# A fused sketched attention and feed-forward kernel: GpSimd's queue, the key products and the task list rearranged

## The chip, the core and the metric

The kernel runs on one core of a Trainium2 chip. Such a core has five engines with a queue of instructions each: PE (TensorE, matrix products), DVE (VectorE), ACT (ScalarE), POOL (GpSimd) and SP (SyncE, which here only issues DMAs). Sixteen DMA engines move data between HBM and the on-chip memory SBUF; PE writes its results to PSUM, which only DVE and ACT read here. The metric is the device time of one execution in microseconds (us), lower is better.

## What is computed

Two parts, one after the other. The attention is linear: each query and key row of 32 numbers is multiplied by two small sketches S1 and S2 (8 x 32), and its 64 features are all products of the 8 numbers of the one with the 8 of the other.

```python
def phi(x):                                        # x: (4, 4, 1088, 32), batch, head, row, 32
    a = einsum('rd,bhsd->bhsr', S1, x)             # 8 numbers per row
    b = einsum('rd,bhsd->bhsr', S2, x)
    return einsum('bhsi,bhsj->bhsij', a, b)        # 64 features
kv  = einsum('bhsf,bhsd->bhfd', phi(k), v)
z   = sum(phi(k), axis=rows)
num = einsum('bhsf,bhfd->bhsd', phi(q), kv)
den = einsum('bhsf,bhf->bhs',  phi(q), z) + 1e-6
x   = (num / den), as 4352 tokens of 4 heads x 32 = 128
h   = x @ w_in                                     # 128 -> 2048
out = (h * sigmoid(h)) @ w_out                     # 2048 -> 128
```

Inputs and output are f32. The second part has 4352 x 2048 silus and two products of 4352 x 128 x 2048.

## The kernel before

The program is a list of small tasks. `ORDER`, a text of entries such as `pk 0 2 4` or `f1 3 5`, names them in the order in which they are written into the program, and each engine works through its own instructions in that order; nothing reorders them. An engine waits at an instruction until all that it depends on is done, and what is behind it waits too. The DMA loads and a few memsets are not in the list: they are written ahead of it, and so stand first in the queues of SP, ACT and POOL.

The attention of each batch b (0 to 3) goes through these tasks. Keys: `kt b` transposes K on DVE; `pk` multiplies by the sketch weights WK on PE; `tk` transposes the result back into SBUF (tile `pk`); `kp b e h` forms the 64 products per key, in four steps of 128 x 576 elements (tile `kp`), all on DVE. `zs`, `zc`, `mm`, `mk` sum the features and put the denominator's weights into a part of the tile WQ. `kv` is the key-value product on PE (with V in bf16, tile `Vb`), and `kw` (on ACT for batch 0, as `kw_act`) masks it by head into KVw. Queries, in pieces of p0 to p1: `qt` transposes, `pq` multiplies by WQ on PE, `tq` transposes back into PQ, `dn` forms and divides by the denominator (four short DVE instructions), `qo` forms the 64 products, `pt` transposes them, `nm` multiplies by KVw on PE, and `xc` copies the attention's result to `xT`, 128 features by token, on ACT (A) or DVE (V).

The feed-forward part goes over ten chunks of tokens (`CHUNKS`: 256, 384, 448, six of 512 and 192). Chunks 0 to 2 are batch 0. `f1 c s` multiplies w_in with a chunk for two (or four, or eight) of the 16 blocks of 128 columns, `sl c s` is the silu on ACT, `f2 c s` adds up the product with w_out in PSUM, and `ot c` transposes and stores. There are two PSUM buffers for `f1` (an H in the list lets a task of the attention use one). `wic i` casts a quarter of w_in to bf16 on ACT, `vc0` casts batch 0's V. `zeros n` are n matrix products with a tile of zeros that nobody reads; they fill PE's time in the start.

`WQ`'s other columns are constants: `wq_const` copies WK into the WQ of the four batches, eight copies on POOL. `L4`, the matrix of `mm`, is made in `weights2`, on DVE.

Loads: K, the first queries and V of batch 0, w_in and the remaining queries are issued by SP without a condition. w_out and V of batches 1 to 3 are issued by POOL, since they are cast to bf16 on the way. `begin(..., after)` makes an issue wait until another transfer has landed:

```python
wo = begin(nc.gpsimd, w_out_bf, moe_w_out.rearrange("(j p) m -> p j m", p=P), wi[1])
prev = q0b
for b in range(1, B):
    load_v(nc.gpsimd, b, Vb[b], prev)
    kb = load_kq(nc.sync, b, k, Kx, after=prev)
    prev = load_kq(nc.sync, b, q, Qx, after=kb)
```

So each K and Q load of batches 1 to 3 is issued when the one before it has landed, and POOL issues the V of a batch when the queries of the batch before have landed.

Of the kernel before, what the change touches and what calls it, by code (L numbers as in the profile page):

```python
# [26 lines left out]
tq 0 10 17, f2 0 0, qo 0 4 10, f1 0 2, pt 0 4 10, sl 0 2
pk 1, dn 0 10 17, nm 0 4 10 H, tk 1, xc 0 4 10 A, kt 2 0 34
f2 0 1, f2 0 2, qo 0 10 17, f1 1 0, sl 1 0, f1 1 4
zs 1, f1 1 2, sl 1 4, f2 0 3, f1 1 1, zc 1 A  # L30
pk 2, sl 1 2, ot 0, pt 0 10 17, sl 1 1, f1 1 6
qt 1 0 34, f2 1 0, f1 1 3, tk 2, mm 1, f2 1 1
sl 1 6, f1 1 5, f2 1 2, mk 1, kp 1 0 1, nm 0 10 17
sl 1 3, pq 1 0 8 H, kp 1 1 1, sl 1 5, xc 0 10 17 A, tq 1 0 8
kp 1 0 0, f1 1 7, kp 1 1 0, f2 1 3, pq 1 8 17, f1 2 0
dn 1 0 8, f2 1 4, sl 1 7, f1 2 4, sl 2 0, kv 1
# [53 lines left out]
def kernel(  # L90
# [157 lines left out]

    def wq_const():
        for b in range(B):  # L250
            nc.gpsimd.tensor_copy(out=WQ[b][:, :, 0:R].rearrange("p h (i e) -> p h e i", e=2),
                                  in_=WK[:, :, 0, :].rearrange("p h (e i) -> p h e i", e=2))
            nc.gpsimd.tensor_copy(out=WQ[b][:, :, R: 2 * R], in_=WK[:, :, 1, :])  # L253

# [26 lines left out]
    def kp(b, e, h):  # L281
        s = t["pk", b][:, :, :, h].rearrange("p n r a i -> p (n r) a i")
        o = t["kp", b][:, :, :, e, h].rearrange("p n r j i -> p (n r) j i")
        nc.vector.tensor_tensor(out=o, in0=bcast(s[:, :, 0, 4 * e: 4 * e + 4], 2, R),  # L284
                                in1=bcast(s[:, :, 1], 3, 4), op=ALU.mult)
# [221 lines left out]
```

## Time and profile before

| | us |
|---|---|
| time, median of 3 runs (range) | 122.09 (121.97 to 122.43) |
| the profiled execution's own time | 121.77 |
| its span, first to last instruction | 119.1 |
| busy: PE, ACT, DVE, POOL | 88.3, 73.3, 67.6, 12.1 |
| 72 silus on ACT, busy | 65.5 |
| 16 key product steps (`kp`) on DVE, busy | 11.3 |
| mean granted TensorE clock | 0.912 of full |

Line numbers such as L352 are those of the kernel before. A row of the timeline gives start, duration, engine, line, operation, the tile written and the tile read with their shapes, the number of instructions that were merged into it, and in brackets how long the engine had stood idle before it and what ended the idle time. A row of the waits gives who waited for whom, the sum in us, how often, and the longest. A row of the groups (line first) gives busy us and the mean duration in ns. A row of the windows gives the stretch, its length, the busy time and the number of instructions of PE, its weight loads, DVE, ACT and POOL, then clock, share of the DMA engines and GB/s. Rows of DMA issues give KB and the us from issue to landing.

### The profile page before, as it was taken

Reading aid. Unit: us, or ns where it says so; the run is one execution under the profiler, and the core shown is the slowest. Engines: PE = TensorE matmul, PEld = TensorE weight load, DVE = VectorE, ACT = ScalarE, POOL = GpSimd, SP = SyncE. Lnnn points to the kernel's source line nnn. Section 1 sums busy time; section 2 is a strip of 40 time slices with the busy share of each in tenths; the row PEclk is TensorE's granted clock in tenths of the full one; section 3 lists DMA queues with packets and bytes.
Section 4 is the critical chain, followed back from the end, with each engine's and each line's share of the span. In section 5 each row is a group of like instructions: output and inputs, shape, how many; then the busy total and the mean of one; then the engine's idle time right before and its main releaser. Section 6 shows DMA issues by size and latency. Waiting matters only on the chain.

```text
span 119.1 us, 2189 instructions
## 1 busy us (share of the span) xinstructions
PE 88.3 (74%) x857; PEld 48.1 (40%) x864; DVE 67.6 (57%) x128; ACT 73.3 (62%) x91; POOL 12.1 (10%) x47
## 2 busy tenths in 40 slices
PE   6499000000089999999999999999999999999920
...
DVE  0349300000048999999999999799398973020210
ACT  2217300000004779969879988999989789999800
...
PEclk9999975555558999999999999999999999999999
...
GB/s 99 288 265 279 125 277 122 151 243 195 148 192 129 6 0 0 44 6 3 66 6 19 61 0 0 90 3 0 88 0 6 47 41 70 18 1 67 21 102 22
DMA packets 24857, 9.81 MB, mean 82 GB/s; under 512 B 21392, under 2 KB 23184, under 8 KB 24848
## 3 DMA queue, kind: packets, MB, share of 16 engines
...
q8 instruction: 6, 0.10, 0.3%
q10 hardware_dynamic: 288, 0.03, 0.2%
q14 instruction: 3, 0.02, 0.1%
...
## 4 chain that ended last, share of the span: by engine, by line
PE 42%; DMA 23%; DVE 17%; ACT 8%; issue 2%; SPq 2%; POOL 2%; POOLq 0%; ACTq 0%; DVEq 0%
PE o_ps L437 18%; PE h_ps L419 16%; DMA Qx<-in_q_dram 11%; DMA Kx<-in_k_dram 9%; ACT g L426 8%; DVE qp L378 3%; DMA T<-in_S_dram 3%; DVE kp L284 2%; DVE PQ L358 2%; PE zps L236 2%; DVE KT L258 2%; SPq L157 2%; POOL Vb L157 2%; PE pq_ps L352 2%; DVE qT L384 1%
## 5 line engine op out<-in xcount | busy, mean ns | idle before, releaser
L426 ACT ACTIVATE g<-h_ps 128x1024 bf16<-128x1024 f32 (+2 forms) x72 | 65.5, 981 | 7.8 <-PE h_ps L419 5.7
L419 PE MATMUL h_ps<-xT,w_in_bf 128*128 128x512 bf16 (+4 forms) x156 | 39.8, 347 | 0.5
L437 PE MATMUL o_ps<-g,w_out_bf 128*128 128x512 bf16 (+4 forms) x157 | 37.5, 346 | 0.4
L437 PEld LDWEIGHTS <-w_out_bf 128*128 128x128 bf16 x160 | 15.2, 98 | 14.5 <-issue 0.7
L419 PEld LDWEIGHTS <-w_in_bf 128*128 128x128 bf16 x160 | 14.2, 98 | 15.2 <-issue 5.6
L352 PE MATMUL pq_ps<-QT,WQ 64*64 64x288 f32 (+3 forms) x48 | 4.0, 409 | 21.6 <-POOL WQ L253 21.6
L358 DVE STREAM_TRANSPOSE PQ<-pq_ps 128x576 f32<-128x576 f32 (+3 forms) x6 | 4.0, 669 | 23.0 <-PE pq_ps L352 23.0
L335 ACT ACTIVATE KVw<-kv_ps,hm 64x64 bf16<-64x64 f32 (+1 forms) x6 | 1.5, 306 | 22.8 <-PE kv_ps L316 22.7
L443 DVE STREAM_TRANSPOSE o_tt<-o_ps 128x512 f32<-128x512 f32 (+4 forms) x10 | 6.3, 635 | 13.9 <-PE o_ps L437 13.8
L236 PE MATMUL zps<-zw 128*128 128x128 bf16 x112 | 10.7, 264 | 1.1 <-POOL hm L196 1.1
L284 DVE TENSOR_TENSOR kp<-pk 128x576 bf16<-128x576 f32 x16 | 11.3, 740 | 0.0
L352 PEld LDWEIGHTS pq_ps<-QT,WQ 64*64 64x64 f32 x48 | 1.4, 143 | 23.4 <-POOL WQ L253 21.7
L236 PEld LDWEIGHTS <-zw 128*128 128x128 bf16 x112 | 9.0, 123 | 3.7 <-issue 2.5
L378 DVE TENSOR_TENSOR qp<-PQ 128x1024 bf16<-128x1024 f32 (+4 forms) x9 | 10.3, 1146 | 0.1
L157 POOL DMA_DIRECT2D Vb<-in_v_dram x12 | 6.5, 546 | 15.2 <-DMA Qx<-in_q_dram 15.2
L384 DVE STREAM_TRANSPOSE qT<-qp 128x512 f32<-128x512 f32 (+4 forms) x9 | 5.9, 659 | 0.1
L258 DVE STREAM_TRANSPOSE KT<-Kx 128x1088 f32<-128x1088 f32 (+2 forms) x5 | 5.3, 1063 | 0.0
L341 DVE STREAM_TRANSPOSE QT<-Qx 128x1088 f32<-128x1088 f32 (+2 forms) x5 | 5.3, 1057 | 0.0
L230 ACT ACTIVATE Vb<-Vx 128x576 bf16<-128x576 f32 x2 | 1.3, 675 | 5.0 <-DMA Vx<-in_v_dram 5.0
L227 DVE CAST xT<-num_ps 128x576 bf16<-128x576 f32 (+1 forms) x5 | 3.6, 714 | 0.2
L271 PE MATMUL h_ps<-KT,WK 64*32 64x288 f32 x16 | 2.4, 682 | 1.8 <-DVE hm L245 1.8
L316 PEld LDWEIGHTS <-kp 128*128 128x128 bf16 x72 | 3.1, 107 | 0.7 <-DVE kp L284 0.2
...
## 6 DMA issues: line engine op xcount, KB each, us to landing
...
w_out_bf<-in_moe_w_out_dram POOLq DMA_DIRECT2D x1, 512.0 KB, 7.0
...
```

The source lines that it names most:

```text
L157: ins = eng.dma_start(dst, src)
L236: nc.tensor.matmul(t["zps"][:, :ncol], zw, zw[:, :ncol], start=True, stop=True)
L258: nc.vector.transpose(out=KT[b % 2][:, y0 * 32: y1 * 32], in_=Kx[b][:, y0:y1, :].rearrange("p a d -> p (a d)"))
L284: nc.vector.tensor_tensor(out=o, in0=bcast(s[:, :, 0, 4 * e: 4 * e + 4], 2, R), in1=bcast(s[:, :, 1], 3, 4), op=ALU.mult)
L352: nc.tensor.matmul(t["pq_ps", b, p0][64 * g: 64 * (g + 1), r, :cols].rearrange("p (y x) -> p y x", x=32), w[rs, :], qv[rs, g, p0:p1, :], s ...
L358: nc.vector.transpose(out=PQ[b % 2][:, p0:p1].rearrange("p y r f -> p r y f"), in_=t["pq_ps", b, p0][:, :, :cols].rearrange("p r (y f) -> ...
L378: nc.vector.tensor_tensor(out=t["qp", b][:, p0:p1].rearrange("p y r j i -> p (y r) j i"), in0=bcast(fa, 2, R), in1=bcast(fb, 3, R), op=ALU ...
L384: nc.vector.transpose(out=dst.rearrange("p r (y x) -> p y r x", x=32), in_=src)
L419: nc.tensor.matmul(h[:, i, :], w_in_bf[:, j * P: (j + 1) * P], xT[:, t0: t0 + ntok], start=True, stop=True)
L426: nc.scalar.activation(out=gv, in_=t.pop(("h", c, s)), func=ACT.Silu)
L437: nc.tensor.matmul(op[c][:, :ntok], w_out_bf[:, j, :], g[:, i, :], start=(j == 0), stop=(j == NJ - 1))
L443: nc.vector.transpose(out=o_tt[:, :ntok], in_=op[c][:, :ntok])
```

## The change

- POOL's queue: V of batches 1 to 3 and w_out are no longer issued ahead of the list, but by tasks in it (`lv b`, `wo`). `wo` waits only for batch 0's V; `lv` for nothing of its own.
- SP: K and Q of batches 1 to 3 are issued without a condition, right behind batch 0's. (The program has eight completion counters for such transfers, used in turn, so an issue waits for the transfer that had its counter before.)
- 11 of the 16 `kp` steps get a P in the list, and run on POOL: two of batch 0, four each of batches 1 and 2, one of batch 3.
- `L4` is made on POOL. The sketches are loaded into 32 rows (T16: two copies of S1 and of S2), and four transposes of 32 x 32 spread them over the partitions; a copy of S2 on all partitions (T2) is kept for L4.
- w_out is loaded with four consecutive rows (2 KB) per partition and group, and w_in's columns are read with a step of four in `wic`, so that the blocks of the two still match.
- The list is another one. `zc` of batch 0 and 1 and `kw` of batch 0 go from ACT to DVE; `zeros` have other counts.

The core of the diff (of the task list, two lines):

```diff
-kp 0 1 1, zeros 13, zs 0, kp 0 0 0, zc 0 A, kp 0 0 1
+kp 0 0 1 P, kp 0 1 1 P, zeros 6, pq 0 0 4, zeros 15, kv 0
...
-    T12 = const.tile([P, 2, D], FP32, name="T12")
-    ST = const.tile([P, 2, 4, R], FP32, name="ST")
+    T16 = const.tile([32, D], FP32, name="T16")
+    T2 = const.tile([P, D], FP32, name="T2")
+    ST = const.tile([P, 2, 2, R], FP32, name="ST")
...
-    sketch(nc.scalar, 0, S1)
-    sketch(nc.scalar, 1, S2)
+    sketch(nc.scalar, T16[0:16, :], S1, 2)
+    sketch(nc.scalar, T16[16:32, :], S2, 2)
...
+    sketch(nc.scalar, T2, S2, P // R)
+    v0 = load_v(nc.sync, 0, Vx)
     for i in range(4):
-        wi.append(begin(nc.sync, w_in_f[:, i * CH:(i + 1) * CH], moe_w_in[:, i * CH:(i + 1) * CH]))
-    q0b = load_kq(nc.sync, 0, q, Qx, 8, NY)
+        begin(nc.sync, w_in_f[:, i * CH:(i + 1) * CH], moe_w_in[:, i * CH:(i + 1) * CH])
+    load_kq(nc.sync, 0, q, Qx, 8, NY)
+    for b in range(1, B):
+        load_kq(nc.sync, b, k, Kx)
+        load_kq(nc.sync, b, q, Qx)
...
-    wo = begin(nc.gpsimd, w_out_bf, moe_w_out.rearrange("(j p) m -> p j m", p=P), wi[1])
-    prev = q0b
-    for b in range(1, B):
-        load_v(nc.gpsimd, b, Vb[b], prev)
-        kb = load_kq(nc.sync, b, k, Kx, after=prev)
-        prev = load_kq(nc.sync, b, q, Qx, after=kb)
...
     def weights():
-        vcopy_in = T12.rearrange("p a d -> p (a d)")
-        nc.vector.transpose(out=ST.rearrange("p a c i -> p (a c i)"), in_=vcopy_in)
-        nc.vector.tensor_tensor(out=WK, in0=ST[:, :, 0:2, :].rearrange("p a h i -> p h a i"),
+        for i in range(4):
+            nc.vector.transpose(out=ST[32 * i: 32 * (i + 1)].rearrange("p a h i -> p (a h i)"), in_=T16)
+        nc.vector.tensor_tensor(out=WK, in0=ST.rearrange("p a h i -> p h a i"),
...
-        nc.vector.tensor_tensor(out=L4, in0=bcast(T12[:, 1, :], 1, H), in1=bcast(hm4, 2, D),
-                                op=ALU.mult)
+        nc.gpsimd.tensor_tensor(out=L4, in0=bcast(T2, 1, H), in1=bcast(hm4, 2, D), op=ALU.mult)
...
+    def wo():
+        begin(nc.gpsimd, w_out_bf.rearrange("p (i e) m -> p i (e m)", e=4),
+              moe_w_out.rearrange("(i p e) m -> p i (e m)", p=P, e=4), v0)
+
+    def lv(b):
+        load_v(nc.gpsimd, b, Vb[b])
...
-    def kp(b, e, h):
+    def kp(b, e, h, eng=nc.vector):
...
-        nc.vector.tensor_tensor(out=o, in0=bcast(s[:, :, 0, 4 * e: 4 * e + 4], 2, R),
+        eng.tensor_tensor(out=o, in0=bcast(s[:, :, 0, 4 * e: 4 * e + 4], 2, R),
...
-    def wic(i, n=4):
-        w = DFF // n
-        acopy(w_in_bf[:, i * w: (i + 1) * w], w_in_f[:, i * w: (i + 1) * w])
+    def wic(i):
+        cols = slice(i * CH, (i + 1) * CH)
+        acopy(w_in_bf[:, cols].rearrange("p (e m) -> p e m", e=4),
+              w_in_f[:, cols].rearrange("p (m e) -> p e m", e=4))
...
-    named = {"A": acopy, "V": vcopy}
+    named = {"A": acopy, "V": vcopy, "P": nc.gpsimd}
```

POOL's queue, right behind its memsets, before. Vb_91 to Vb_93 are V of batches 1 to 3, WQ_98 is batch 0's WQ; a bracket names the counters of the engines and transfers that the instruction waits for (DMAHW transfers of SP and ACT, DMASW those of POOL):

```order
L157 DMA w_out_bf<-in_moe_w_out_dram 128x16x128 [waits DMAHW2_49]
L157 DMA Vb_91<-in_v_dram 32x4x288 [waits DMAHW5_49]
L157 DMA Vb_91<-in_v_dram 32x4x288 x2
L157 DMA Vb_91<-in_v_dram 32x4x224
L157 DMA Vb_92<-in_v_dram 32x4x288 [waits DMAHW7_49]
L157 DMA Vb_92<-in_v_dram 32x4x288 x2
L157 DMA Vb_92<-in_v_dram 32x4x224 [waits DMASW0_49]
L157 DMA Vb_93<-in_v_dram 32x4x288 [waits DMAHW1_49,DMASW1_49]
L157 DMA Vb_93<-in_v_dram 32x4x288 [waits DMASW2_49]
L157 DMA Vb_93<-in_v_dram 32x4x288 [waits DMASW3_49]
L157 DMA Vb_93<-in_v_dram 32x4x224 [waits DMASW4_49]
L251 COPY WQ_98<-WK 128x2x2x4 [waits DVE_49,Pool_49]
```

The same place now; kp_229, kp_483 and kp_564 are the products of batches 0, 1 and 2 (between the first copies and the last stand those of the other WQ):

```order
L242 TENSOR_TENSOR L4_120<-T2_117,hm4_123 128x128 [waits DMAHW4_49,DVE_49,Pool_49]
L246 COPY WQ0_98<-WK_119 128x2x2x4
L248 COPY WQ0_98<-WK_119 128x2x8
...
L286 TENSOR_TENSOR kp_229<-pk_228 128x18x32 [waits DVE_49]
L286 TENSOR_TENSOR kp_229<-pk_228 128x18x32
L158 DMA w_out_bf_114<-in_moe_w_out_dram 128x4x512 [waits DMAHW1_49]
L158 DMA Vb1_91<-in_v_dram 32x4x288 x3
L158 DMA Vb1_91<-in_v_dram 32x4x224
L158 DMA Vb2_92<-in_v_dram 32x4x288 x3
L158 DMA Vb2_92<-in_v_dram 32x4x224 [waits DMASW0_49]
L286 TENSOR_TENSOR kp_483<-pk_482 128x18x32 [waits DVE_49]
L286 TENSOR_TENSOR kp_483<-pk_482 128x18x32 x3
```

The copies into WQ moved from behind all twelve V loads to ahead of every load, behind L4; two product steps stand ahead of w_out, and the V of batch 3 (not shown) behind all eleven.

DVE's queue from the key products of batch 0 to the first use of its KVw, before (PQ_106 is the transposed query product; `kw` of this batch was on ACT):

```order
L284 TENSOR_TENSOR kp<-pk 128x18x32 x3
L306 TENSOR_TENSOR WQ_98<-m_ps,hm_120 128x2x2x4
L284 TENSOR_TENSOR kp<-pk 128x18x32
L358 STREAM_TRANSPOSE PQ_106<-pq_ps 128x2x4x32
L368 TENSOR_TENSOR AW_108<-PQ_106 128x8x8
L369 TENSOR_REDUCE DN_110<-AW_108 128x8
L370 RECIPROCAL DN_110<-DN_110 128x8
L371 TENSOR_TENSOR PQ_106<-PQ_106,DN_110 128x8x8
L341 STREAM_TRANSPOSE QT_96<-Qx_85 128x832
L378 TENSOR_TENSOR qp<-PQ_106 128x512
L384 STREAM_TRANSPOSE qT<-qp 128x4x2x32
L358 STREAM_TRANSPOSE PQ_106<-h_ps 128x2x6x32
```

And now, from the second product step on:

```order
L286 TENSOR_TENSOR kp<-pk 128x18x32
L308 TENSOR_TENSOR WQ_98<-m_ps,hm_121 128x2x2x4
L360 STREAM_TRANSPOSE PQ_106<-pq_ps 128x2x4x32
L370 TENSOR_TENSOR AW_108<-PQ_106 128x8x8
...
L380 TENSOR_TENSOR qp<-PQ_106 128x512
L386 STREAM_TRANSPOSE qT<-qp 128x4x2x32
L327 TENSOR_TENSOR KVw_102<-kv_ps,hm_121 128x128
L330 TENSOR_TENSOR KVw_102<-kv_ps,hm_121 64x128 x2
L343 STREAM_TRANSPOSE QT_96<-Qx_85 128x832
L223 CAST xT<-num_ps 128x256
L360 STREAM_TRANSPOSE PQ_106<-h_ps 128x2x6x32
```

Two of the four product steps left DVE's queue here; the three masks of `kw` and the copy of `xc` came in, and the long transpose of the remaining queries moved behind them.

More of the change, by code (lines that the diff above doesn't have):

```diff
@@ L27 @@
[L27 to L36, printed above, removed]
@@ L78 @@
-ot 8, f2 9 0, f2 9 1, sl 9 3, f2 9 2, f2 9 3
-ot 9
+weights, vc0 0 2, vc0 2 4, kt 0 0 18, kt 0 18 34, qt 0 0 8
+zeros 33, pk 0 0 2 H, zeros 3, pk 0 2 4, weights2, tk 0
+wq_const, kp 0 0 0, zeros 13, zs 0, zc 0 V, zeros 5
+mm 0, wic 1, wic 0, kp 0 1 0, mk 0, wic 2
+kp 0 0 1 P, kp 0 1 1 P, zeros 6, pq 0 0 4, zeros 15, kv 0
+tq 0 0 4, dn 0 0 4, qo 0 0 4, pt 0 0 4, kw 0, zeros 23
+nm 0 0 4, qt 0 8 34, wic 3, xc 0 0 4 V, wo, zeros 11
+pq 0 4 10 H, f1 0 0, tq 0 4 10, dn 0 4 10, qo 0 4 10, sl 0 0
+pq 0 10 17, f1 0 1, zeros 2, f1 0 2, pt 0 4 10, f2 0 0
@@ new lines @@
+dn 1 0 8, f1 2 1, f1 2 0, sl 2 1, mm 2, kp 2 0 1 P
+pk 3, kp 2 1 1 P, sl 2 0, f1 2 4, f2 1 6, f1 2 3
+mk 2, sl 2 4, kp 2 0 0 P, qo 1 0 8, tk 3, sl 2 3
+kv 1, f1 2 7, sl 2 7, kw 1, pt 1 0 8, f2 1 7
+f1 2 2, pq 1 8 17, nm 1 0 8 H, ot 1, xc 1 0 8 V, zs 3
+sl 2 2, kp 2 1 0 P, tq 1 8 17, f1 2 6, f2 2 0, f1 3 0
+f2 2 1, f2 2 2, sl 2 6, sl 3 0, f1 3 2, sl 3 2
+qt 2 0 34, f2 2 3, dn 1 8 17, f1 2 5, pq 2 0 8, sl 2 5
+f1 3 6, f2 2 4, sl 3 6, kp 3 0 0, f1 3 7, qo 1 8 17
+zc 3 V, f2 2 5, sl 3 7, pt 1 8 17, tq 2 0 8, f2 2 6
@@ new lines @@
+f1 3 1, sl 3 1, f2 2 7, ot 2, f1 3 4, sl 3 4
+kv 2, f1 3 5, f2 3 0, nm 1 8 17 H, sl 3 5, pq 2 8 17
+f1 3 3, dn 2 0 8, f2 3 1, xc 1 8 17 V, f1 4 1, f2 3 2
+sl 3 3, kw 2, f1 4 0, qo 2 0 8, kp 3 1 1 P, sl 4 1
+f2 3 3, pt 2 0 8, f1 4 4, kp 3 0 1, sl 4 0, f2 3 4
+f1 4 3, sl 4 4, sl 4 3, f2 3 5, f2 3 6, f1 4 7
+f2 3 7, tq 2 8 17, sl 4 7, f1 4 6, sl 4 6, mm 3
+nm 2 0 8, ot 3, f1 4 2, sl 4 2, f2 4 0, f1 4 5
+qt 3 0 34, f2 4 1, lv 3, xc 2 0 8 V, f1 5 4, sl 4 5
+f2 4 2, f2 4 3, sl 5 4, mk 3, f1 5 0, f2 4 4
@@ new lines @@
+sl 5 0, f1 5 5, dn 2 8 17, pq 3 0 8, qo 2 8 17, pt 2 8 17
+kp 3 1 0, sl 5 5, f1 5 2, f2 4 5, f1 5 6, f2 4 6
+sl 5 2, tq 3 0 8, sl 5 6, nm 2 8 17, f1 5 1, dn 3 0 8
+f2 4 7, sl 5 1, f1 5 3, sl 5 3, xc 2 8 17 V, pq 3 8 17
+f1 6 2, ot 4, sl 6 2, tq 3 8 17, f2 5 0, f1 5 7
+f2 5 1, sl 5 7, f2 5 2, f1 6 0, sl 6 0, dn 3 8 17
+f2 5 3, f2 5 4, qo 3 8 17, f1 6 5, f2 5 5, qo 3 0 8
+f1 6 6, sl 6 5, kv 3, kw 3, f1 6 7, pt 3 0 8
+f2 5 6, sl 6 6, f1 6 1, f2 5 7, sl 6 7, ot 5
+f1 6 4, nm 3 0 8, sl 6 1, xc 3 0 8 V, sl 6 4, f1 6 3
```

85 lines of the change are left out of this document (28 added, 57 removed).

## Prediction

> **What bounds the kernel now.** I read the slices first, to see whether one engine is the limit all the way, then the waits, then the timeline around the longest one. On the page, each digit is a fortieth of the span, 2.98 us:
>
> ```profile
> span 119.1 us, 2189 instructions
> PE   6499000000089999999999999999999999999920
> DVE  0349300000048999999999999799398973020210
> ACT  2217300000004779969879988999989789999800
> PEclk9999975555558999999999999999999999999999
> ```
>
> All three engines stand still in slices 5 to 10. After that PE is full to slice 38. The kernel is thus 39 us of start and 75 us of dense work, and the start is mostly a hole. The waits name what closes it:
>
> ```profile
> PE pq_ps L352 <- POOL WQ L253: 21.6, 1, 21.6
> POOL Vb L157 <- DMA Qx<-in_q_dram: 15.2, 3, 7.9
> ```
>
> The first query product (`pq`, L352) wants the constant columns of WQ, copied by GpSimd (POOL). The timeline shows why the copies are late:
>
> ```profile
> 9.15 0.78 DVE L278 STREAM_TRANSPOSE pk<-h_ps 128x576 f32<-128x576 f32 x1 [1.86 <-PE h_ps L271]
> 9.91 1.29 POOL L157 DMA_DIRECT2D w_out_bf<-in_moe_w_out_dram  x1 [5.56 <-DMA w_in_f<-in_moe_w_in_dram]
> 9.97 2.10 DVE L284 TENSOR_TENSOR kp<-pk 128x576 bf16<-128x576 f32 x3
> 11.98 0.17 DVE L306 TENSOR_TENSOR WQ<-m_ps,hm 128x16 f32<-128x16 f32 x1
> 12.59 2.16 POOL L157 DMA_DIRECT2D Vb<-in_v_dram  x4 [1.38 <-DMA Qx<-in_q_dram]
> ...
> 30.71 2.15 POOL L157 DMA_DIRECT2D Vb<-in_v_dram  x4 [5.90 <-DMA Qx<-in_q_dram]
> 32.90 0.20 POOL L251 COPY WQ<-WK 128x16 f32<-128x16 f32 x1
> 33.28 0.70 PE L352 MATMUL pq_ps<-QT,WQ 64*64 64x128 f32 x8 [21.57 <-POOL WQ L253]
> ```
>
> The copies stand in GpSimd's queue behind twelve V loads, and those wait for the chain of K and Q loads. DVE's own part of WQ was done at 12.15. The chain of work shows the loads one behind the other (544 KB each):
>
> ```profile
> 12.30 6.78 DMA Kx<-in_k_dram
> 19.10 3.28 DMA Qx<-in_q_dram
> ```
>
> The dense part, from the first `f1` to the end:
>
> ```profile
> 39.23 1.04 PE L419 MATMUL h_ps<-xT,w_in_bf 128*128 128x256 bf16 x8
> 39.87 3.77 ACT L426 ACTIVATE g<-h_ps 128x1024 bf16<-128x1024 f32 x4 [0.70 <-PE h_ps L419]
> 59.22 0.68 DVE L227 CAST xT<-num_ps 128x512 bf16<-128x512 f32 x1
> 59.96 0.38 PE L419 MATMUL h_ps<-xT,w_in_bf 128*128 128x512 bf16 x1
> 71.60 0.69 PE L316 MATMUL kv_ps<-Vb,kp 128*128 128x64 bf16 x18
> 113.93 0.38 DVE L443 STREAM_TRANSPOSE o_tt<-o_ps 128x192 f32<-128x192 f32 x1 [1.70 <-PE o_ps L437]
> ```
>
> Batch 0 (chunks 0 to 2) is worked off from 39.23 to 59.96, 20.7 us, while DVE makes batch 1; the rest takes 119.1 - 59.96 = 59.1 us.
>
> **The hole.** Now the copies follow `L4` on GpSimd, which needs the sketches and one DVE reduction: both are there by 8 us (pk itself is transposed at 9.15), and eight copies of 0.20 end before DVE's part of WQ. No load stands ahead of them. The chain that sets the first `f1` is then DVE's, and its steps have these durations:
>
> ```profile
> 34.05 0.45 DVE L358 STREAM_TRANSPOSE PQ<-pq_ps 128x256 f32<-128x256 f32 x1 [21.24 <-PE pq_ps L352]
> 34.54 0.22 DVE L368 TENSOR_TENSOR AW<-PQ 128x64 f32<-128x64 f32 x1
> 35.51 1.04 DVE L341 STREAM_TRANSPOSE QT<-Qx 128x832 f32<-128x832 f32 x1
> 36.47 0.65 DVE L378 TENSOR_TENSOR qp<-PQ 128x512 bf16<-128x512 f32 x1
> 37.16 0.45 DVE L384 STREAM_TRANSPOSE qT<-qp 128x256 f32<-128x256 f32 x1
> 37.29 0.56 PE L352 MATMUL h_ps<-QT,WQ 64*64 64x192 f32 x8
> 38.79 0.39 ACT L230 ACTIVATE xT<-h_ps 128x256 bf16<-128x256 f32 x1 [1.67 <-PE h_ps L393]
> L325 DVE TENSOR_TENSOR KVw<-kv_ps,hm 128x128 bf16<-128x128 f32 x3 | 0.8, 263 | 0.0
> L328 DVE TENSOR_TENSOR KVw<-kv_ps,hm 64x128 bf16<-64x128 f32 x6 | 1.7, 289 | 0.2
> ```
>
> The four steps of the quotient (`dn`) take 35.51 - 34.54 = 0.97.
>
> **A key product step on GpSimd.** No row shows it: 576 elements, two operands read, one written. The nearest rows:
>
> ```profile
> L284 DVE TENSOR_TENSOR kp<-pk 128x576 bf16<-128x576 f32 x16 | 11.3, 740 | 0.0
> L207 POOL MEMSET Vx<- 32x256 f32 x1 | 0.3, 307 | 0.1
> L196 POOL MEMSET hm<- 128x2 f32 x1 | 0.1, 101 | 0.0
> L251 POOL COPY WQ<-WK 128x16 f32<-128x16 f32 x4 | 0.8, 200 | 0.0
> L203 POOL TENSOR_SCALAR_AFFINE_SELECT E<-E 128x8 f32<-128x8 f32 x1 | 0.2, 193 | 0.1
> ```
>
> The memsets give 0.1 us and (307 - 101)/254 = 0.81 ns for each element written. Three streams of that make 0.1 + 576 x 2.43 ns = 1.5 us. The lower end is DVE's 0.74. The copy, at (200 - 100)/16 = 6.2 ns, would give 3.7; the select, at 93/8 = 11.6 ns, 6.8, but eight elements are nearly all overhead. I take 1.5, from the row with most elements, and keep 0.74 and 3.7. The Trainium skill, GPSIMD Engine Reference, section 3.1, states about 2.6 cycles per element for a two-input operation at 1.2 GHz; an estimate from that page is 1.25 us, and the sum below would be some 1 us lower by it. No run here shows it yet.
>
> **Does it hinder DVE?** The two steps of batch 0 now start beside DVE's other two, and batch 1's four beside `dn` and `qo`. One end is no hindrance: above, GpSimd's 1.29 us beside three `kp` leaves them 2.10/3 = 0.70 each. But there GpSimd wrote descriptors and read no tile. The other end is that two instructions that each read two tiles take turns. I take turns, since the only row that shows them together is of another kind, and keep overlap as a rival. The rule that speaks against the change is in the Trainium skill, SBUF — State Buffer, "Who interferes with whom": a DVE instruction with two SBUF inputs and a GpSimd instruction that reads SBUF use one shared port, and the second to issue is blocked until the first has finished. By the row alone the sum would be 98.9, by the rule 103.4; no trace here decides yet.
>
> **The first f1, step by step.** pk is there at 9.93, as before. DVE step to 10.67, GpSimd's to 12.17, DVE's second to 12.91, DVE's part of WQ (0.17) 13.08, `pq` (0.56) 13.64, `tq` (0.45) 14.09; GpSimd's second runs 12.91 to 14.41, and `dn` waits for it: 15.38. `qo` 16.03, `pt` 16.48, `kw`, now on DVE (0.26 + 2 x 0.29), 17.32, `qt` 18.36, second `pq` (PE) 18.92, beside it `xc` (0.39). First `f1` at 18.9 for 39.23: -20.3. The key-value product lies beside it (14.41 + 0.7, before `kw`), and so do the zeros on PE.
>
> **Batch 0 worked off.** From `kt 1` (38.42) to the end of `xc 1` (59.90) DVE took 21.5 us with hardly a gap. Counted by the order, the same stretch gains 2.95 us (first `tq`, `zt`, third `kt`, one WQ, third pk) and loses 4.95 (four `kp`, and `tq` and `dn` of batch 1's second half): 19.5, or 19.3 from the first `f1`. Four GpSimd steps in it, each keeping DVE half a step, 4 x 0.75 = 3.0: 22.3 against 20.7, +1.6. GpSimd itself: pk of batch 1 is there at about 25.8, and four steps with DVE's turns between end near 35, a microsecond or two before DVE comes to `kw 1`. That cover is thin, and the next thing late without it.
>
> **Loads.** `w_out` is now issued behind GpSimd's second step, at 14.4, and not at 9.9:
>
> ```profile
> w_out_bf<-in_moe_w_out_dram POOLq DMA_DIRECT2D x1, 512.0 KB, 7.0
> 7.00:12.30 5.30, 4.71 (x85) 3.15 (x81) 3.41 (x7) 2.99 (x7) 1.29 (x1) 1.00 0.80 269
> ```
>
> With the same 7.0 us it lands at 21.4; `f2` of chunk 0 comes at about 21.1 (three `f1`, a `pq` and the first silu): +0.3. Rows of 2 KB for 512 bytes may shorten it; more transfers beside it may lengthen it. After 12.3 there are six K and Q loads (3.3 MB), V (1.7) and `w_out` (1.0 in f32); at the 269 GB/s of the full stretch that is 22 us, all landed by 35; batch 3's K is wanted by DVE then. On SP nothing is delayed by the free order: output stores stand behind. V of batches 1 and 2 is issued by 20 and wanted near 35; V of batch 3 stands behind the eleventh step and is wanted last.
>
> **Small parts.** Four 32-row transposes for one of 0.246: 0 to +0.7, at nothing, since three zeros fewer on PE give back 0.4 ahead of the second `pk`. `w_in` read in steps of four: 0.62 each as before, 6 us ahead of its use. `zt` and `kw` change engines inside the chains above.
>
> **The rest**, 59.1 us, I leave: the silus of ACT there and PE's matmuls are unchanged, and DVE has less. Bounds -1 and +2.
>
> Sum: 119.1 - 20.3 + 1.6 + 0.3 = 100.7 us of span. The profiled execution took 121.77, 2.7 outside the span: 103.4. It stands 0.3% below the median of 122.09; half a per cent is what this measurement tells from no change.
>
> **Rivals.**
> 1. No hindrance: first `f1` at 17.1 (-22.1), batch 0 worked off in 19.3 (-1.4), `w_out` +0.6: 96.2 + 2.7 = 98.9. For it: the 0.70 row. Chance 0.22.
> 2. Loads in the way: `w_out` queues behind all K and Q, 3.3 MB at 269 GB/s or 12.3 us, and lands 5 us later; PE holds `f2` and all behind it: 108.4. For it: that K load took 6.78 us beside `w_out` and V, the next 3.28. Chance 0.13.
> 3. A step takes 3.7: first `f1` at 23.3 (-15.9), four half steps 7.4 (+6.0), +0.3: 112.2. Chance 0.10.
> 4. Slower than before: GpSimd bounds. Batch 2's product stands at 71.60 now; eight steps from 25.8 reach it at (71.6 - 25.8)/8 = 5.7 us a step, and above that the kernel loses. Only the eight-element select speaks for it. Chance 0.02.
> 5. The copies stay late, because `L4` ahead of them is: its sketch would have to land after 30. Nothing speaks for it; 0.01.
>
> The forecast has 0.50, between 101 and 106; 0.02 is for what I don't see. The range runs from rival 1 to rival 2, 98.5 to 108.5, and leaves out rival 3's end. All but rivals 4 and 5 are faster: 0.97, same 0.01, slower 0.02.
>
> **What would show it.** WQ copies before 11 us and `pq` near 13.5; no half clock in slices 6 to 12. A GpSimd `kp` of 1.5 us, with DVE's `kp` or `dn` idle or stretched beside it. First `f1` at 18.9, `f1` of chunk 3 near 41, then 59 to the end. Wrong if a step takes over 2.5 us, if `f2` of chunk 0 waits over 2 us for `w_out`, or if `kt 3` waits for its load.

## The result, and the profile after

The changed kernel took 108.33 us (median of 4 runs, 107.23 to 110.07); before took 122.03 beside it (121.22 to 122.43). The ratio is 0.882, with a 95% interval of 0.873 to 0.890. The forecast was 103.4: the direction was right, but the time missed the 101 to 106 that the forecast itself had, and came out at the upper end of the range, where rival 2 (loads in the way, 108.4) stood. Here and below a time is the median of all runs, and a ratio leaves out the slow runs, those over 1.5% above the fastest of their kernel, here 110.07 and 108.90 and in e3_all_dve one of 296.64. The profiled execution took 107.76, with a span of 106.1.

The page of the changed kernel, in fortieths of the span (2.65 us each):

```profile
span 106.1 us, 2183 instructions
PE   5809998935999995899999999999999999999900
DVE  0063769898299999999379499989792050020210
ACT  0505950280999397158979999989899999998500
POOL 6605699402099993900000000000000000000000
PEclk9999999999999999759999999999999999999998
GB/s 48 295 198 281 374 420 415 330 210 121 24 0 44 15 0 0 45 139 4 0 85 8 0 59 43 0 2 97 0 6 54 45 36 63 0 25 65 43 89 23
```

The long hole is gone. A short one is left on PE in slices 8 and 9 (it stands from 22.2 to 25.0 us), ACT is weak up to slice 17, and the transfers run at 374 to 420 GB/s in slices 4 to 6 and are done by slice 10. The timeline (rows picked from it) shows what the short hole is:

```profile
10.27 0.19 POOL L248 COPY WQ<-WK 128x16 f32<-128x16 f32 x1
10.72 0.78 DVE L280 STREAM_TRANSPOSE pk<-h_ps 128x576 f32<-128x576 f32 x1 [1.89 <-PE h_ps L273]
14.18 0.45 PE L354 MATMUL pq_ps<-QT,WQ 64*64 64x128 f32 x8 [0.24 <-DVE WQ L308]
14.93 0.94 POOL L158 DMA_DIRECT2D w_out_bf<-in_moe_w_out_dram  x1
19.86 0.61 PE L421 MATMUL h_ps<-xT,w_in_bf 128*128 128x256 bf16 x4
25.02 1.05 PE L439 MATMUL o_ps<-g,w_out_bf 128*128 128x256 bf16 x8 [2.84 <-DMA w_out_bf<-in_moe_w_out_dram]
28.42 0.79 DVE L280 STREAM_TRANSPOSE pk<-pk_ps 128x576 f32<-128x576 f32 x1 [2.17 <-PE pk_ps L273]
45.02 1.06 PE L421 MATMUL h_ps<-xT,w_in_bf 128*128 128x512 bf16 x2
```

The copies of WQ end at 10.46, the first `pq` waits only for DVE's part of WQ, and the first `f1` comes at 19.86 instead of 39.23. But `f2` of chunk 0 waits 2.84 us for `w_out`, issued at 14.93 and landed near 25. PE stands, and its queue holds the key product of batch 1 behind `f2`. DVE waits 2.17 us for that product. The `f1` of chunk 3, at 45.02, ran at a low clock (windows; the columns behind the busy times are the granted clock, the share of the DMA engines and GB/s):

```profile
45.00:48.00 3.00, 3.00 (x11) 1.19 (x10) 2.90 (x7) 1.51 (x2) 0.00 (x0) 0.61 0.98 128
```

### The profile page after: what moved, and what is told of

The parts are those of the page before. It is cut to its first block, busy times and chain, and to the rows that moved or that the text cites. A ratio compares the mean times of both kernels' runs of the same rounds, so it can differ in the third digit from the quotient of the medians.

```text
span 106.1 us, 2183 instructions
## 1 busy us (share of the span) xinstructions
PE 91.2 (86%) x863; PEld 48.0 (45%) x863; DVE 65.3 (62%) x125; ACT 73.3 (69%) x82; POOL 26.9 (25%) x59
## 4 chain that ended last, share of the span: by engine, by line
PE 60%; DVE 15%; DMA 13%; POOL 3%; issue 3%; ACTq 1%; DVEq 0%
PE o_ps L439 26%; PE h_ps L421 24%; DMA w_out_bf<-in_moe_w_out_dram 9%; DMA T<-in_S_dram 4%; POOL kp L286 3%; DVE KT L260 3%; DVE pk L280 3%; PE h_ps L273 2%; PE pq_ps L354 2%; DVE o_tt L445 1%; PE num_ps L395 1%; DVE qT L386 1%; ACTq L178 1%; PE h_ps L395 1%; DVE AW L370 1%
## 5 line engine op out<-in xcount | busy, mean ns | idle before, releaser
L439 PE MATMUL o_ps<-g,w_out_bf 128*128 128x512 bf16 (+4 forms) x160 | 39.2, 355 | 3.0 <-DMA w_out_bf<-in_moe_w_out_dram 2.8
L421 PE MATMUL h_ps<-xT,w_in_bf 128*128 128x512 bf16 (+4 forms) x160 | 41.4, 352 | 0.1
L286 POOL TENSOR_TENSOR kp<-pk 128x576 bf16<-128x576 f32 x11 | 14.9, 1378 | 6.5 <-DVE pk L280 6.5
L232 PE MATMUL zps<-zw 128*128 128x128 bf16 x111 | 10.5, 264 | 1.1 <-POOL hm L199 1.1
L380 DVE TENSOR_TENSOR qp<-PQ 128x1024 bf16<-128x1024 f32 (+4 forms) x9 | 11.2, 1257 | 0.2
L360 DVE STREAM_TRANSPOSE PQ<-pq_ps 128x512 f32<-128x512 f32 (+3 forms) x8 | 5.5, 684 | 1.1 <-PE pq_ps L354 1.0
L354 PE MATMUL pq_ps<-QT,WQ 64*64 64x256 f32 (+3 forms) x64 | 5.1, 391 | 1.0 <-DVE pk L280 0.8
L226 ACT ACTIVATE w_in_bf<-w_in_f 128x512 bf16<-128x512 f32 x4 | 4.2, 1116 | 1.0 <-DMA w_in_f<-in_moe_w_in_dram 1.0
L236 DVE STREAM_TRANSPOSE ST<-T 32x32 f32<-32x32 f32 x4 | 0.8, 202 | 6.1 <-DMA T<-in_S_dram 6.0
L286 DVE TENSOR_TENSOR kp<-pk 128x576 bf16<-128x576 f32 x5 | 3.9, 789 | 0.0
L280 DVE STREAM_TRANSPOSE pk<-pk_ps 128x576 f32<-128x576 f32 x3 | 2.3, 763 | 2.2 <-PE pk_ps L273 2.2
```

What stands on the lines that cost most here:

```text
L232: nc.tensor.matmul(t["zps"][:, :ncol], zw, zw[:, :ncol], start=True, stop=True)
L286: eng.tensor_tensor(out=o, in0=bcast(s[:, :, 0, 4 * e: 4 * e + 4], 2, R), in1=bcast(s[:, :, 1], 3, 4), op=ALU.mult)
L354: nc.tensor.matmul(t["pq_ps", b, p0][64 * g: 64 * (g + 1), r, :cols].rearrange("p (y x) -> p y x", x=32), w[rs, :], qv[rs, g, p0:p1, :], s ...
L360: nc.vector.transpose(out=PQ[b % 2][:, p0:p1].rearrange("p y r f -> p r y f"), in_=t["pq_ps", b, p0][:, :, :cols].rearrange("p r (y f) -> ...
L380: nc.vector.tensor_tensor(out=t["qp", b][:, p0:p1].rearrange("p y r j i -> p (y r) j i"), in0=bcast(fa, 2, R), in1=bcast(fb, 3, R), op=ALU ...
L421: nc.tensor.matmul(h[:, i, :], w_in_bf[:, j * P: (j + 1) * P], xT[:, t0: t0 + ntok], start=True, stop=True)
```

## The experiments

Twelve kernels were run in three sets of four, in the order of the table, each set beside before. Before took 122.71, 121.53 and 122.63 beside them, and the changed kernel was timed apart, beside 122.03. So kernels of different sets are compared by their ratios to before, where 0.01 is 1.2 us. "f2" is the first second-layer matmul, "chunk 3" the first `f1` of chunk 3 in the profiled execution; the landing is `w_out`'s, from its issue.

| kernel | edit | time | ratio to before (95%) | first f1 | w_out issue + landing | f2 | chunk 3 |
|---|---|---|---|---|---|---|---|
| after | the change | 108.33 | 0.882 (0.873 to 0.890) | 19.86 | 14.93 + 10.0 | 25.02 | 45.02 |
| e1_queue | before, loads issued behind the WQ copies | 103.38 | 0.840 (0.834 to 0.847) | 17.36 | 10.77 + 6.7 | 19.51 | 42.24 |
| e2_wo_first | after, `w_out` ahead of GpSimd's steps | 105.45 | 0.857 (0.850 to 0.864) | 19.02 | 9.65 + 13.8 | 23.52 | 44.52 |
| e3_all_dve | after, 16 steps on DVE | 108.11 | 0.875 (0.868 to 0.882) | 19.96 | 10.16 + 14.0 | 24.16 | 46.28 |
| e4_old_sketch | after, before's sketches | 107.97 | 0.882 (0.875 to 0.889) | 19.36 | 14.32 + 10.1 | 24.42 | 46.56 |
| e5_free | e1, K and Q loads free | 106.63 | 0.880 (0.873 to 0.887) | 18.12 | 10.33 + 14.7 | 25.07 | 45.37 |
| e9_k1_free | e1, K of batch 1 free | 102.53 | 0.845 (0.839 to 0.851) | 17.55 | 10.28 + 7.3 | 19.70 | 39.68 |
| e6_chain | after, K and Q loads in order | 106.65 | 0.878 (0.874 to 0.882) | 18.10 | 13.09 + 6.8 | 20.25 | 43.81 |
| e7_old_rows | after, before's `w_out` and `w_in` rows | 108.57 | 0.891 (0.883 to 0.898) | 19.68 | 14.57 + 10.6 | 25.24 | 47.35 |
| e13_k1_free_after | after, loads as in e9 | 103.84 | 0.847 (0.840 to 0.853) | 17.57 | 12.65 + 7.4 | 20.14 | 42.52 |
| e14_all_dve | e13, 16 steps on DVE | 106.02 | 0.864 (0.857 to 0.871) | 18.85 | 9.63 + 8.6 | 21.01 | 43.84 |
| e11_gp8 | e9, 8 steps on GpSimd | 111.20 | 0.904 (0.896 to 0.912) | 18.05 | 10.42 + 8.7 | 20.19 | 49.91 |
| e12_k2_early | e9, K of batch 2 behind `w_out` | 100.76 | 0.819 (0.811 to 0.827) | 17.32 | 10.23 + 8.1 | 19.47 | 40.26 |

### One edit of the queue: e1_queue

```diff
-wic 1, wq_const, wic 0, zeros 10, mm 0, mk 0
+wic 1, wq_const, loads, wic 0, zeros 10, mm 0, mk 0
+    def loads():   # w_out, and V, K and Q of batches 1 to 3, with the same waits
```

> The kernel before, with one edit: the eight constant copies into WQ stand on GpSimd ahead of the w_out and V issues instead of behind them (those issues now follow them, under the same waits; the K and Q loads keep their chain). Theory: this queue order alone is the 20 us hole. The first f1 should come at 17.5 to 19 us instead of 39.2; batch 1 then meets its loads (K of batch 1 landed at 19.1, of batch 2 at 26.0), which costs 2 to 5 us before chunk 3; rest as before. Span 100 to 103, time 103 to 106, so as fast as the full change or faster. Rival: the other parts of the change (free loads, GpSimd product steps) carry part of the gain: then the first f1 is early but chunk 3 starts past 48 us, and the time is above 109.

103.38, ratio 0.840: the whole gain and more, with before's list, engines, rows and load chain. This shows the cause of the hole: it was GpSimd's queue that held the WQ copies, and moving the loads behind them closes it without the rest of the change. What e1 still waits for is the chain of loads:

```profile
17.36 1.04 PE L420 MATMUL h_ps<-xT,w_in_bf 128*128 128x256 bf16 x8
19.51 0.60 PE L438 MATMUL o_ps<-g,w_out_bf 128*128 128x256 bf16 x4
19.61 1.31 DVE L259 STREAM_TRANSPOSE KT<-Kx 128x1088 f32<-128x1088 f32 x1 [2.73 <-DMA Kx<-in_k_dram]
```

### Why w_out is late: e2, e5, e9

e2 moves one word, `wo`, ahead of `kp 0 0 1 P`.

> The changed kernel, with w_out issued on GpSimd ahead of the two product steps of batch 0 instead of behind them (about 10.4 us instead of 14.9). Theory: the 2.8 us for which PE waited for w_out at the first f2, and the 2.2 us for which DVE then waited for pk of batch 1, go to the end one to one: PE no longer waits there, span shorter by 2.2 to 2.8, about 105.5 to 106. Rival: DVE's chain of batch 1 (turns with GpSimd, then the slow clock) sets chunk 3 anyway: chunk 3 still starts at about 45 us and the time stays within 0.7 us of 108.3.

```profile
9.65 0.93 POOL L158 DMA_DIRECT2D w_out_bf<-in_moe_w_out_dram  x1
23.52 1.11 PE L439 MATMUL o_ps<-g,w_out_bf 128*128 128x256 bf16 x8 [2.18 <-DMA w_out_bf<-in_moe_w_out_dram]
```

Issued 5.3 us earlier, `w_out` still landed only 1.5 us earlier. So its landing hardly follows its issue. The time fell by what the theory had said (105.45, ratio 0.857 against 0.882), but not by its route. PE still waited 2.18, and DVE transposed pk of batch 1 at 28.44, where the changed kernel did it at 28.42. Of the 2.4 us by which the span is shorter, 0.5 lie ahead of chunk 3 and 1.9 behind it, where e2's granted clock is 1.00 from 45 to 48 us and the changed kernel's 0.61:

```profile
28.44 0.78 DVE L280 STREAM_TRANSPOSE pk<-pk_ps 128x576 f32<-128x576 f32 x1 [3.04 <-PE pk_ps L273]
45.00:48.00 3.00, 3.00 (x21) 1.25 (x20) 2.90 (x7) 2.89 (x4) 0.00 (x0) 1.00 0.82 112
```

e5 and e9 change only waits of loads in e1:

```diff
e5: -            kb = load_kq(nc.sync, b, k, Kx, after=prev)
    -            prev = load_kq(nc.sync, b, q, Qx, after=kb)
    +            load_kq(nc.sync, b, k, Kx)
    +            prev = load_kq(nc.sync, b, q, Qx)
e9: -            kb = load_kq(nc.sync, b, k, Kx, after=prev)
    +            kb = load_kq(nc.sync, b, k, Kx, after=None if b == 1 else prev)
```

> e1_queue with one more edit: the K and Q loads of batches 1 to 3 no longer wait for one another; V and w_out wait as before. Theory (too many loads at once make w_out late): the 2.7 us wait of KT for K of batch 1 goes, but w_out lands 10 us or more after its issue instead of 6.7, the first f2 begins 2.5 to 4 us later than 19.5, and the two nearly cancel: 102.5 to 104.5. Rival (free loads cost nothing, the lateness in the changed kernel has to do with its own w_out or list): w_out lands in 7, the wait of KT is gone, 100.0 to 101.5.

> e1_queue with K of batch 1 alone free of the chain, so that it is issued near 6.7 us instead of 12.8; the rest stays in order. Theory: 0.5 MB more before w_out makes w_out about 1 us later (landing near 8), the wait of KT for K of batch 1 (2.7 us, to 19.6) is gone, net 1.5 to 2.5 us less than e1_queue: 101 to 102. Rival (batch 0's work sets the end and not KT): 103.4, as e1_queue.

Free loads made e1 slower, by more than either theory said (106.63, ratio 0.880 against 0.840). Freeing one load alone is 4.1 us better than that in the same set (102.53, half a us above its theory's bound). Against e1 it shows no gain (ratio 0.845 against 0.840, with overlapping intervals). In the profiles its last transpose ends 2.6 us earlier (94.04, in e1 96.60), but e9 needs 6.3 us from there to the end and e1 4.7. The `f2` of e5 and e9, and e9's key transpose that still waits:

```profile
25.07 1.04 PE L438 MATMUL o_ps<-g,w_out_bf 128*128 128x256 bf16 x4 [4.64 <-DMA w_out_bf<-in_moe_w_out_dram]
```

```profile
19.70 0.60 PE L438 MATMUL o_ps<-g,w_out_bf 128*128 128x256 bf16 x4
24.09 1.31 DVE L259 STREAM_TRANSPOSE KT<-Kx 128x1088 f32<-128x1088 f32 x1 [1.08 <-DMA Kx<-in_k_dram]
```

The first row is e5's, the other two e9's. With the loads free, `w_out` landed between 23.4 and 25.2 in six kernels (after, e2, e3, e4, e5, e7), whether issued at 9.65 or at 14.93. The packets of each queue show two reasons (packets, MB, share of the 16 engines; q1 carries SP's loads, q0 GpSimd's `w_out` and V). First the changed kernel from 14 to 20 us, then e13, whose loads stand in order:

```profile
q1 hardware_dynamic: 610, 2.37, 97.1%
q0 software_dynamic: 47, 0.05, 4.7%
```

```profile
q0 software_dynamic: 927, 0.73, 87.7%
q1 hardware_dynamic: 83, 0.35, 16.1%
```

The first reason is a late start. Counted in quarters of a us, GpSimd's queue moved its first packet at 19.0 in the changed kernel. In the six kernels with free loads that is 4.1 to 4.4 us after the issue of `w_out`; with the loads in order it is 1.6 to 2.9 us (3.6 in e14). From its first packet on, `w_out` took 5.9 us in the changed kernel and 5.8 in e13. So between these two the late start is the whole difference; what the queue waits for, no run shows.

The second reason shows where the two queues move together for long. e2, then e5, from 16 to 20 us:

```profile
q1 hardware_dynamic: 266, 1.03, 68.6%
q0 software_dynamic: 267, 0.27, 40.3%
```

```profile
q1 hardware_dynamic: 350, 1.37, 90.3%
q0 software_dynamic: 351, 0.09, 21.9%
```

The queues moved equal numbers of packets (266 and 267, 350 and 351), but K's and Q's packets are 3.9 KB on average and `w_out`'s 1.0 KB in e2 and 0.26 KB in e5 (0.27 MB / 267, 0.09 MB / 351). In these stretches the engines are shared by packets, not by bytes, and the queue of small rows gets a fifth of the bytes in e2 and a sixteenth in e5. The Trainium skill, DMA: Bandwidth & Descriptors, section "SWDGE vs HWDGE vs iDMA", says that each DMA engine goes round between its queues and changes only at packet boundaries; the counts of e2 and e5 agree with it, and the changed kernel's 610 to 47 do not speak against it, since its first packets came only at 19.0.

### The same on the changed kernel: e6, e7, e4

```diff
e6: -    load_kq(nc.sync, 0, q, Qx, 8, NY)
    +    prev = load_kq(nc.sync, 0, q, Qx, 8, NY)
     ...
    +        kb = load_kq(nc.sync, b, k, Kx, after=prev)
    +        prev = load_kq(nc.sync, b, q, Qx, after=kb)
e7: w_out_bf[:, j, :] loaded by rows j*128 + p, w_in_bf copied without steps, as before
e4: T12 and one 128x64 transpose, as before
```

> The changed kernel with the loads of K and Q of batches 1 to 3 in before's order again, each waiting for the one ahead. Theory (crowd of loads): w_out lands about 7 us after its issue near 15, so near 22, the first f2 waits at most 0.5 us and comes near 22 instead of 25.0, the f1 of chunk 3 near 43; 105 to 106.5, unless KT of batch 1 then waits for K (in e1_queue 2.7 us). Rival (w_out is late because of its own rows and queue): landing 10 again, f2 at 25, 107.8 to 108.8.

`w_out` landed in 6.8 and `f2` came at 20.25 without a wait, yet the time shows no clear gain (106.65, ratio 0.878 against 0.882, with overlapping intervals). Now DVE waits 4.0 us for K and Q between the first `f1` and chunk 3, which takes 25.7 us, in the changed kernel 25.2. K of batch 2 is the first that is late, and PE runs at a lower clock behind it (0.86 from 30 to 40 us):

```profile
20.25 1.25 PE L439 MATMUL o_ps<-g,w_out_bf 128*128 128x256 bf16 x8
27.87 1.31 DVE L260 STREAM_TRANSPOSE KT<-Kx 128x1088 f32<-128x1088 f32 x1 [1.61 <-DMA Kx<-in_k_dram]
```

> The changed kernel with before's layout of w_out (16 groups of 128 rows, one row of 256 bytes a time) and before's plain copies of w_in. Theory (the rows matter little beside the crowd): packets of the software queue back to 3792, w_out lands as late or up to 3 us later, the four ACT copies of w_in 0.62 us each instead of 1.12 and still beside other work; 108.0 to 110. Rival (groups of four rows are what makes w_out late): it lands in 7, f2 near 22, 105 to 106.

108.57, so the rows made no difference that the intervals separate: 10.6 for the landing instead of 10.0, although GpSimd's queue now has 3792 packets and not 2256. The copies of `w_in` (groups of after, then of e7) show what the steps of four cost ACT, beside other work:

```profile
L226 ACT ACTIVATE w_in_bf<-w_in_f 128x512 bf16<-128x512 f32 x4 | 4.2, 1116 | 1.0 <-DMA w_in_f<-in_moe_w_in_dram 1.0
```

```profile
L226 ACT ACTIVATE w_in_bf<-w_in_f 128x512 bf16<-128x512 f32 x4 | 2.4, 625 | 1.2 <-DMA w_in_f<-in_moe_w_in_dram 1.2
```

> The changed kernel with the sketches loaded and transposed as before (both on all 128 partitions, one transpose of 128x64). Theory: the new sketch load (landed 6.0 instead of 4.8 us) and its four transposes (0.85 instead of 0.25) put the whole start back by 1.6 to 1.9 us, and w_out with it, since it is issued behind the product steps: first f1 at about 18.0 instead of 19.9, time about 106.5. Rival: K, w_in and w_out set the start, so less than 0.5 us comes of it.

No gain (107.97), as the rival said. Its own first transpose still waited until 6.02:

```profile
6.02 0.24 DVE L233 STREAM_TRANSPOSE ST<-T 128x64 f32<-128x64 f32 x1 [6.02 <-DMA T<-in_S_dram]
```

So the sketch's late landing (4.75 before) does not come from its new form alone. It was there at 4.8 to 5.4 us in the seven kernels with ordered loads and at 5.2 to 6.0 in the six with free ones, though the free loads are issued only from 7.7 on. Why stays open.

### GpSimd's steps: e3, e13, e14, e11

> The changed kernel with all 16 product steps on DVE, in the same list (w_out is then issued right behind the WQ copies, at about 10.4). Theory that the two engines take turns, so that GpSimd's steps give DVE little: the four steps of batch 1 cost DVE 3.0 us and give back the 2 us or so of its stretched instructions, w_out no longer waits (-2.5): about 106 to 107. DVE's quotient and qp of batch 1 are then 0.28 and 1.23 us again (0.88 and 2.08 with GpSimd). Rival that GpSimd's steps relieve DVE by their full 0.74 each: batch 1 and batch 2 are later by 3 us each, 109 to 111.

> The changed kernel, its K and Q loads in the order of e9_k1_free: K of batch 1 free, the others one behind the other. Theory (in the changed kernel the freed loads cost more than they bring): w_out issued near 13, landed near 21, first f2 near 20.5 to 21.5 instead of 25.0, no long wait of KT for K of batch 1, f1 of chunk 3 near 42.5; 104 to 105.5, better than e6_chain (106.65). Rival (the list and GpSimd cost the rest, loads nothing beyond e6_chain): 106.5.

> e13_k1_free_after with all 16 key product steps on DVE. Theory (steps on the two engines take turns, so GpSimd brings nothing): within 0.7 us of e13_k1_free_after. Rival (GpSimd relieves DVE of 11 x 0.74 = 8 us, part of it on the path now that w_out is in time): 1.5 to 4 us slower than e13_k1_free_after. A third (GpSimd's steps are late): 1 us or more faster.

> e9_k1_free with the eight key product steps of batches 1 and 2 on GpSimd instead of DVE. Theory (turns): DVE loses 8 x 0.74 = 5.9 us of work and gets longer neighbours back; GpSimd needs about 1.3 us a step; 102 to 103.5, so no gain on e9_k1_free (102.53). Rival (overlap): 100 to 101.5. Rival (late): the steps end later, kv 1 and the query products of batch 1 wait, 104 or more.

e3 and e14 take the `P` off every `kp`, e11 puts it on the eight of batches 1 and 2 in before's list; e13 has e9's edit. In the changed kernel the steps were worth nothing that the intervals separate (e3 108.11 beside 108.33, ratio 0.875 against 0.882). DVE's quotient and `qp` came back to 0.29 and 1.22 us as e3's theory said, but PE still waited 1.89 for `w_out`. In the profiles chunk 3 comes 1.3 later in e3, and what follows it is 1.9 shorter, as in e2. With `w_out` in time, e14 is 2.2 us slower than e13 in the same set (106.02 beside 103.84), as its rival said. Eight steps on GpSimd cost e11 some 7 us (ratio 0.904 against e9's 0.845), as the rival of late steps said. So no single price holds. The rows show what each engine does to the other. A GpSimd step (duration min/median/max), in the changed kernel:

```profile
L286 POOL TENSOR_TENSOR kp<-pk x11: 1167/1222/2125, 11.6 to 41.5; 128x576 bf16<-128x576 f32 x11
```

In batch 0 the steps take turns. First e13, two steps on each engine, then e14, all four on DVE:

```profile
9.25 0.76 DVE L286 TENSOR_TENSOR kp<-pk 128x576 bf16<-128x576 f32 x1
9.30 3.40 POOL L286 TENSOR_TENSOR kp<-pk 128x576 bf16<-128x576 f32 x2
10.01 1.65 DVE L286 TENSOR_TENSOR kp<-pk 128x576 bf16<-128x576 f32 x1
```

```profile
10.21 0.76 DVE L286 TENSOR_TENSOR kp<-pk 128x576 bf16<-128x576 f32 x1
11.60 0.75 DVE L286 TENSOR_TENSOR kp<-pk 128x576 bf16<-128x576 f32 x1
12.35 1.42 DVE L286 TENSOR_TENSOR kp<-pk 128x576 bf16<-128x576 f32 x2
```

On two engines the four steps last 3.45 us (9.25 to 12.70), on one 3.56 (10.21 to 13.77), a wait of DVE for the zt product included. DVE's second step takes 1.65 for 0.75, and GpSimd's two 1.70 each for 1.17. In the later batches GpSimd does take work off DVE, since much of DVE's work there is transposes, which no row shows stretched. From the first `f1` to chunk 3 (columns PE, PEld, DVE, ACT, POOL) DVE is busy 21.25 us in e13 and 24.22 in e14:

```profile
17.57:42.52 24.95, 20.68 (x312) 11.07 (x309) 21.25 (x39) 16.27 (x21) 13.60 (x14) 1.00 0.59 146
```

```profile
18.85:43.84 24.99, 20.53 (x313) 11.37 (x310) 24.22 (x46) 16.37 (x21) 2.39 (x5) 1.00 0.51 135
```

But the stretch is equally long, 24.95 and 24.99 us: e13's DVE waits 2.8 us for K in it, and e14's for no load. Of the 1.4 us between the two spans (102.0 and 103.4), 1.3 stand already at the first `f1`, and 1.0 of these at pk, transposed at 8.43 and not at 9.39, before any step. There the sketch landed 0.4 earlier, and e14's granted clock was 0.79 from 5 to 10 us. So in these two profiles at most 0.4 us can be GpSimd's, and why the medians are 2.2 apart is not shown.

In e11 all eight steps ran in one row, and held one DVE instruction all the while:

```profile
31.78 9.40 DVE L369 TENSOR_TENSOR AW<-PQ 128x128 f32<-128x128 f32 x1
31.92 9.10 POOL L285 TENSOR_TENSOR kp<-pk 128x576 bf16<-128x576 f32 x8
36.54 1.14 PE L317 MATMUL kv_ps<-Vb,kp 128*128 128x64 bf16 x18 [3.00 <-POOL kp L285]
```

The same operation takes 0.28 us in before. The key-value product, too, came 4 us later than e9's (32.50), but DVE came back only at 41.2, and with it everything that waits for DVE. The stretch from the first `f1` to chunk 3 takes 31.9 us, in e9 22.1, and this one row is 9.1 us longer than the operation alone.

### A faster version: e12_k2_early

```diff
-            kb = load_kq(nc.sync, b, k, Kx, after=None if b == 1 else prev)
+            kb = load_kq(nc.sync, b, k, Kx, after=(None, wo, prev)[b - 1])
```

> e9_k1_free with K of batch 2 waiting for w_out (landed near 17.6) instead of Q of batch 1 (20.5). Theory: the wait of KT for K of batch 2 (1.08 us at 24.1) is gone and nothing else moves: 101.3 to 102.2. Rival (Q of batch 1 then lands later and QT waits for it, or the wait was not on the path): 102.5 to 103.5.

100.76, ratio 0.819 (0.811 to 0.827), the fastest kernel here, and below the ranges of both the theory and the rival. But it did not come about as expected: DVE's wait for K of batch 2 grew, and its last transpose ends no earlier than e9's (e9, then e12):

```profile
93.66 0.38 DVE L444 STREAM_TRANSPOSE o_tt<-o_ps 128x192 f32<-128x192 f32 x1 [1.71 <-PE o_ps L438]
```

```profile
24.68 1.31 DVE L259 STREAM_TRANSPOSE KT<-Kx 128x1088 f32<-128x1088 f32 x1 [1.88 <-DMA Kx<-in_k_dram]
94.25 0.38 DVE L444 STREAM_TRANSPOSE o_tt<-o_ps 128x192 f32<-128x192 f32 x1 [1.70 <-PE o_ps L438]
```

What made e12's runs shorter (e9's ratio is 0.845) is not in these two traces. The two kernels ran in different sets, and their spans differ in the time from the last transpose to the end: 6.3 us in e9 and 4.7 in e12, 6.0 in e6 and 4.1 to 5.1 in all others. The cause stays open.

## Why the prediction was right, and where not

- **The hole.** Right in cause: WQ copies by 10.5, no half clock in slices 6 to 12, and e1 shows that the queue alone does it. First `f1` 19.86 for 18.9.
- **Small parts at nothing (0 to +0.7).** Wrong by more than the bound: pk was ready at 11.50 for 9.93, so 1.6 late. The four transposes cost 0.85 for 0.25; the rest is the sketch, which landed 1.3 later (some of that came back before pk).
- **A step, 1.5 us.** It measured 1.17 at least and 1.22 in the middle, and 1.70 beside DVE; from pk to `pq` 2.68 us passed where the sum had 3.15. The Trainium skill, GPSIMD Engine Reference, section 3.1, gave an estimate of 1.25 us: the median of 1.22 agrees.
- **Turns.** Right for two-operand instructions. In batches 1 and 2 four DVE rows of the changed kernel are stretched, the longest ones

```profile
36.47 0.88 DVE L370 TENSOR_TENSOR AW<-PQ 128x128 f32<-128x128 f32 x1
38.57 2.08 DVE L380 TENSOR_TENSOR qp<-PQ 128x1024 bf16<-128x1024 f32 x1
```

  against 0.28 and 1.22 alone; with two of PQ (0.54 and 0.53 for 0.29) that is 2.0 us where the sum had 3.0, although eight GpSimd steps ran in the stretch and not the four of the sum. e13 and e14 confirm the turns for batch 0. The Trainium skill, SBUF — State Buffer, "Who interferes with whom", says that the second to issue waits until the first has finished; here that holds step by step, but e11's instruction began 0.14 us ahead of the first GpSimd step and waited for eight of them, which the rule does not give.
- **Loads: the step that failed.** "With the same 7.0 us it lands at 21.4; +0.3." It landed in 10.0, at 24.9, and `f2` came at 25.02 for 21.1, with a wait of 2.84 where the prediction called itself wrong from 2 on. "On SP nothing is delayed by the free order" was true of SP's queue and missed what the crowd does to GpSimd's: 4.1 us until its first packet. The text named this case as rival 2, at 0.13, with 5 us of delay; 3.5 came. e13 takes the crowd away and leaves the rest of the change as it is: 103.84, ratio 0.847 against 0.882. That is 0.4 from the forecast of 103.4, but by luck, since its spans do not put the gain where `w_out` waited. Its batch 0 still took 24.95 us (17.57 to 42.52) and not 22.3: DVE waits 2.8 there for K of batches 2 and 3, which the order makes late. Its first `f1` came 2.3 earlier, half of it from the sketch and half from the first key product on PE, which in the changed kernel ran slowly (the second half of it, in after and in e13):

```profile
9.47 1.18 PE L273 MATMUL h_ps<-KT,WK 64*32 64x288 f32 x8
```

```profile
7.68 0.69 PE L273 MATMUL h_ps<-KT,WK 64*32 64x288 f32 x8
```

  And its rest was 1.6 shorter. That the kernel with free loads is slower is shown by the edit, here and in e5 beside e9. By how much is not: in the changed kernel the sketch had landed (6.04) and the key product begun (7.92) before the first freed load was issued, at 8.24, so the 2.3 us need not be the loads', and how much of the rest is `w_out` is open too. Rival 2 should have had the larger chance: the row that spoke for it (a K load of 6.78 us beside `w_out` and V, 3.28 alone) was the only row of two queues at work together, and it showed a doubling.
- **Batch 0 worked off, 22.3.** From the first `f1` to chunk 3 it took 25.2 (window):

```profile
19.86:45.02 25.16, 20.64 (x313) 11.42 (x310) 22.27 (x40) 16.43 (x21) 14.15 (x14) 0.98 0.40 63
```

  DVE was busy 22.27 us of it, the sum's 22.3, though by luck: the turns cost 1.0 less and its other work took 1.0 more. The difference is what the sum had left out, the 2.17 for which DVE waited for the key product behind `f2`, and smaller gaps. But to take the wait for `w_out` away does not bring 22.3: e6 and e14, whose `f2` waits for nothing, took 25.7 and 25.0, and the eight kernels with the changed list 25.0 to 27.7. e9, whose DVE waits only 1.1, took 22.1 with before's list and all steps on DVE.
- **The rest, 59.1 (-1, +2).** 61.1 in the changed kernel, with a clock of 0.61 at its start; 59.5 (102.0 - 42.5) in e13 and 59.2 in e2, where the clock is full there. The clock itself was not tested.
- **Outside the span.** 107.76 - 106.1 = 1.7 for 2.7, which gave 1.0 back; nothing in the prediction foresaw that.

Together: +1.0 (hole), +2.9 (batch 0), +2.0 (rest) and -0.5 (the 0.3 for `w_out`, and rounding) make 5.4 more span than 100.7, and 4.4 more time.
